# Sharing the odd half-tile of the last product between two batches, and four column groups for a one-column DFT

## The chip, the cores and the metric

One core of one Trainium2 chip. The metric is device time in microseconds (us) of one launch. Eleven executions of the kernel before in one set of rounds lay between 1286.47 and 1290.47 us, 0.3% apart, in another between 1286.91 and 1292.74, 0.5%. All runs quoted here were graded fast. In profile lines PE is the matmul engine (PEld its weight loads), DVE is VectorE, ACT is ScalarE, POOL is GpSimd, SP issues DMA transfers; L89 is line 89 of the kernel. The *granted clock* is the share of its full speed at which PE was let run.

## The reference, cut to what matters

```python
X = np.fft.fft(np.fft.fft(x, axis=1), axis=2).real       # x: (8, 3136, 256), float32
h = np.maximum(X @ w_in, 0.0)                             # 256 -> 1024
conv = sum(conv_w[k] * hp[:, k:k + 3136, :] for k in range(3))   # 3 taps along the sequence, hp is h padded
out = (h * (1 / (1 + np.exp(-conv)))) @ w_out             # 1024 -> 256
```

(The convolution is a loop in the original.) The kernel does the sequence DFT with matmuls on folded input and uses the mirror symmetry of the real part: a first product gives h for a position and its mirror image.

Of the kernel before, what the change touches and what calls it, by code (L numbers as in the profile page):

```python
# [34 lines left out]
def kernel(  # L35
# [34 lines left out]
    ebp = ctx.enter_context(tc.tile_pool(name="ebp", bufs=5))  # L70
    asp = ctx.enter_context(tc.tile_pool(name="asp", bufs=2))
# [167 lines left out]
    def units(b):  # L239
# [5 lines left out]
        def even(sn, c):  # L245
            n = HO // 2 + 1 - c
            nh = HO // 2
            cols = slice(c, HE, 2)
            mms = [product((slice(0, P), slice(j * n, (j + 1) * n)), w(2 * sn + c), sn, q, cols, q == qs[0], q == qs[1])
                   for j, qs in enumerate(((3, 1), (2, 0))) for q in qs]  # L250

            def copy(p):
                a_[sn, c] = asp.tile([P, HO], F32, name="as", tag="as")
                nc.scalar.copy(out=a_[sn, c][:, 0:n], in_=p[:, 0:n])

            def fin(p):
                a, bb, t = a_[sn, c], p[:, n:2 * n], PQ[b][sn]
                vt(t[:, 2 * c:Q4 + 1:4], a[:, 0:n], bb, op=ALU.add)
                hi = t[:, M - 2 * c:Q4:-4]
                x0, x1 = (bb[:, 0:nh], a[:, 0:nh]) if sn else (a[:, 0:nh], bb[:, 0:nh])  # L260
                vt(hi, x0, x1, op=ALU.subtract)
            return Unit(b, mms, copy, fin)
# [4 lines left out]
        def odd_even(sn):  # L267
# [3 lines left out]
            def copy(p):  # L271
                a_[sn] = asp.tile([P, HO + QO], F32, name="as", tag="ao")
                nc.scalar.copy(out=a_[sn][:, HO:], in_=p[:, 0:QO])

            def fin(p):
                a, e0, e2 = a_[sn], a_[sn][:, HO:], p[:, QO:2 * QO]
                vt(a[:, 0:QO], e0, e2, op=ALU.add)
                x0, x1 = (e2, e0) if sn else (e0, e2)
                vt(a[:, HO - 1:QO - 1:-1], x0, x1, op=ALU.subtract)
# [14 lines left out]
        def feature():  # L294

            mms = []
            for j, qs in enumerate(((3, 1), (2, 0))):
                for q in qs:
                    for c in range(2):
                        n = HO // 2 + 1 - c  # L300
                        mms.append(product(
                            (slice(32 * c, 32 * c + 1), slice(j * n, (j + 1) * n)),
                            lambda k, q, c=c: ea[b][0:k, c, q:q + 1], 0, q, slice(c, HE, 2), q == qs[0], q == qs[1]))

            def copy(p):
                a_["e"] = asp.tile([P, HO + QO], F32, name="as", tag="ao"), asp.tile([P, HO], F32, name="as", tag="as")
                for c in range(2):
                    n = 2 * (HO // 2 + 1 - c)
                    nc.scalar.copy(out=a_["e"][c][0:1, 0:n], in_=p[32 * c:32 * c + 1, 0:n])
# [22 lines left out]
    def spread(b):  # L332

        for c, ch in enumerate(chunks):
            eb[b, c] = ebp.tile([P, HN], F32, name="eb", tag="eb")[:, 0:ch.k1 - ch.k0]
            nc.sync.dma_start(out=eb[b, c], in_=ed[b:b + 1, ch.k0:ch.k1].to_broadcast([P, ch.k1 - ch.k0]))

# [4 lines left out]
    class Chunk:  # L342
        def __init__(self, c):
            c0 = CUTS[c]
            c1 = CUTS[c + 1] if c + 1 < len(CUTS) else NK
            self.k0, self.k1 = max(c0 - 1, 0), min(c1 + 1, NK)
            n = self.k1 - self.k0
            f0 = 1 if c0 == 0 else 0
            self.front = slice(f0, f0 + n)
            b0, b1 = (1 if c0 == 0 else 0), (n - 1 if c1 == NK else n)  # L350
            self.cols = slice(b0, b1)
            self.back = slice(f0 + n, f0 + n + b1 - b0)
            self.zeros = c0 == 0
            self.w = self.back.stop + (1 if c0 == 0 else 0)
            if c1 == NK:
                runs = [(0, c0, S - 2 * c0 + 1)]
            else:
                runs = [(0, c0, c1 - c0), (f0 + n, S - c1 + 1, c1 - max(c0, 1))]
            self.tiles = [(g + i, r + i, min(P, l - i)) for g, r, l in runs for i in range(0, l, P)]

    chunks = [Chunk(c) for c in range(len(CUTS))]
    HW = max(c.w for c in chunks)
    HN = max(c.k1 - c.k0 for c in chunks)

# [110 lines left out]
    def copies(s):  # L475
# [4 lines left out]
        for i, cols in enumerate((slice(0, n), ch.cols)):  # L480
            act(nb[s][:, i, cols], p[:, cols], AF.Copy, scale=-1.0 if i else 1.0)  # L481

    def combine(s):
# [7 lines left out]
        for i, (to, cols) in enumerate(((h[:, ch.front], slice(0, n)), (h[:, ch.back][:, ::-1], ch.cols))):  # L491
# [13 lines left out]

    def sigmoid(s):

        n = gs[s].shape[1]
        for c in (slice(n // 2, n), slice(0, n // 2)):
            act(gs[s][:, c], gs[s][:, c], AF.Sigmoid)  # L510

    def gate(s):

        g, h = gs[s], hs.pop(s)
        n = g.shape[1]
        m = n // 2
        gt(g[:, m:n], g[:, m:n], h[:, m + 1:n + 1], op=ALU.mult)  # L517
        vt(g[:, 0:m], g[:, 0:m], h[:, 1:m + 1], op=ALU.mult)  # L518

    def mm2(s):  # L520
        b, c, f = s
        tiles = chunks[c].tiles
        for i, (o, r, m) in enumerate(tiles):
            if f == 0 and i % 2 == 0:
                po[b, c, i // 2] = pso.tile([P, 2, D], F32, name="po", tag="po")
            pt = po[b, c, i // 2]
            mm(pt[0:m, i % 2, :], gs[s][:, o:o + m], wout[:, f, :],
               f == 0 and i % 2 == 0, f == NF - 1)
            if f == NF - 1 and (i % 2 or i == len(tiles) - 1):
                del po[b, c, i // 2]  # L530
                osb = osp.tile([P, 2, D], F32, name="os", tag="os")
                for j in range(i - i % 2, i + 1):
                    _, r, m = tiles[j]
                    nc.scalar.copy(out=osb[0:m, j % 2], in_=pt[0:m, j % 2])  # L534
                    nc.sync.dma_start(out=rows[b * S + r:b * S + r + m, :], in_=osb[0:m, j % 2])
# [10 lines left out]
    for i, u in enumerate(us):  # L546
# [5 lines left out]
        if i == 4:  # L552
            spread(0)
# [18 lines left out]
    for b in range(1, B):  # L572
# [22 lines left out]
        at(cs[-1] - 2, "load", lambda b=b: spread(b))  # L595
# [100 lines left out]
```

## The kernel before: what the change and the argument touch

The kernel is a software pipeline of 256 *steps* (8 batches x 4 chunks of the sequence x 8 groups of 128 hidden features). In each cycle a step's first product runs on PE, the next ones have their taps and gates, and the last product (`po`) of the step three behind runs on PE. The DFT of the next batch is cut in units that are slipped in between.

```python
for t in range(n + LAG):                      # cut: guards
    sigmoid(steps[t - 2])                     # ScalarE, two halves
    products(steps[t + 1]); copies(steps[t + 1])
    run("act")                                # a DFT unit's copies out of PSUM (ScalarE)
    combine(steps[t])                         # VectorE: h of a position and of its mirror
    run("load")                               # loads of x
    run("dve")                                # a DFT unit's sums, the row transfer, POOL's row work
    ...
    other_taps(steps[t - 1])                  # VectorE
    gate(steps[t - 2])                        # h * sigmoid: one half on POOL, one on VectorE
    mm2(steps[t - LAG])                       # PE: the last product
    run("pe")                                 # a DFT unit's matmuls
```

A batch's last product has 3136 rows. The kernel before cuts them into 25 tiles: 23 of 128 rows, one of 127 and one of 65. (With the cut of the chunks moved by a column, as in the change, they are 24 of 128 and one of 64.) Feature D/2 of the DFT is one column that fits in no other unit; its sums are done on POOL in one partition ("row work"):

```python
def feature():                                # one column of weights, two column groups of PE
    for j, qs in enumerate(((3, 1), (2, 0))):
        for q in qs:
            for c in range(2):                # cut: the operands
                mms.append(product((slice(32 * c, 32 * c + 1), slice(j * n, (j + 1) * n)), ...))
    def copy(p):                              # ScalarE, two copies
        for c in range(2):
            nc.scalar.copy(out=a_["e"][c][0:1, 0:n], in_=p[32 * c:32 * c + 1, 0:n])
    def fin(p):                               # POOL, 1 partition
        for c in range(2):
            gt(t[:, 2 * c:Q4 + 1:4], a, bb, op=ALU.add)
            gt(t[:, M - 2 * c:Q4:-4], a[:, 0:nh], bb[:, 0:nh], op=ALU.subtract)
        nc.gpsimd.tensor_scalar(out=t[:, 3:NK:4], in0=t[:, 3:NK:4], scalar1=-1.0, ...)
        nc.sync.dma_start(out=ed[b:b + 1, :], in_=t)
def row():                                    # a 6 KB transfer that POOL's sums are added beside
    nc.sync.dma_start(out=er[b], in_=PQ[b][1][P - 1:P, :])
```

Note the order: row work is issued in `run("dve")`, ahead of `gate` in the same cycle. All of the row work and half of the gate are on POOL, which takes them in this order: in batch 4 the row work from 777.22 us on, the gate at 783.02.

## Time and profile before

| | before |
|---|---|
| time | 1289.94 us, median of 3 |
| span of the profiled execution | 1288.0 us |
| start-up until the first step | 81.4 us |
| batches 1 to 6, from the start of one to the start of the next | 146 to 152 us |

The prediction shows the busy lines and the stretches that it uses. In lists of waits the columns are total idle time, number of times and the longest. This is the list of what PE waited for in the kernel before; the columns are total idle time, number of times and the longest:

```profile
PE po L89 <- DVE g L518: 13.7, 27, 1.6
PE po L89 <- POOL g L517: 12.7, 10, 2.1
```

PE waits nearly as long for POOL's half of the gate, in only ten places, as for VectorE's half in twenty-seven. In seven of the ten (11.4 us) POOL's row work stands in front of the gate; the other three, 0.4 us each, come a step later.

### The profile page before, as it was taken

To read this page: it belongs to the slowest core of one execution; us is meant where nothing else is said; L and a number is where in the kernel's file an instruction comes from. 1 tells how busy PE (TensorE), PEld (TensorE's weight loads), DVE (VectorE), ACT (ScalarE), POOL (GpSimd) and SP (SyncE) were. 2 spreads that over 40 slices of the span, in tenths; PEclk is the share of its full clock that TensorE was granted. 3 is DMA by queue.
4 is the path that set the end of the run, shared out by engine and by line. 5 is a ranking of instruction groups with operands and counts; after the bars stand their busy time and mean duration, and the time that the engine had idled before them with its cause. 6 is when DMAs were issued, how large, how long until landed. Compare 5 with 4: busy or idle time off the path is not lost.

```text
span 1288.0 us, 15443 instructions
## 1 busy us (share of the span) xinstructions
PE 1198.0 (93%) x4914; PEld 898.6 (70%) x4914; DVE 1153.2 (90%) x1664; ACT 880.2 (68%) x1814; POOL 404.1 (31%) x507
## 2 busy tenths in 40 slices
PE   0758999999999999999999999999999999999998
PEld 0535677777677766777677776777677777777776
DVE  6869998998989988898899988998999878898996
ACT  0216766777668766777667776777767777777885
POOL 2414524241523334232513225141322213222222
PEclk9868999999999999999999999999999999999999
DMA  7701202020211102020202103020010001100101
GB/s 226 191 26 39 88 26 87 13 78 25 88 38 44 55 30 76 25 78 25 72 29 63 40 25 100 26 77 5 22 50 26 27 25 44 32 6 22 33 26 44
DMA packets 46842, 66.04 MB, mean 51 GB/s; under 512 B 5600, under 2 KB 35196, under 8 KB 46504
## 3 DMA queue, kind: packets, MB, share of 16 engines
q1 hardware_dynamic: 41012, 49.80, 12.5%
q0 software_dynamic: 5120, 12.85, 3.4%
q10 hardware_dynamic: 628, 2.40, 0.6%
q8 instruction: 38, 0.62, 0.2%
q14 instruction: 44, 0.36, 0.1%
HBM read 39.24 MB, written 25.74 MB: 50 GB/s over the span
## 4 chain that ended last, share of the span: by engine, by line
PE 69%; DVE 17%; issue 4%; ACT 4%; DMA 3%; POOL 2%; DVEq 0%; SPq 0%; ACTq 0%; POOLq 0%
PE po L89 43%; PE pb L89 10%; PE pa L89 9%; PE pd L89 7%; DVE g L504 4%; DVE h L492 2%; DVE g L518 2%; ACT nb L481 2%; DMA dm<-dft_dim_dram 1%; POOL er L319 1%; DVE w L174 1%; DVE xh L147 1%; DVE w L175 1%; DVE xh L158 1%; ACT g L510 1%
## 5 line engine op out<-in xcount | busy, mean ns | idle before, releaser
L89 PE MATMUL po<-wout,g 128*128 128x256 f32 (+2 forms) x3200 | 740.1, 381 | 26.6 <-DVE g L518 13.7
L89 PEld LDWEIGHTS po<-wout,g 128*128 128x128 f32 (+2 forms) x3200 | 597.3, 188 | 190.4 <-DVE g L518 43.4
L504 DVE SCALAR_TENSOR_TENSOR g<-h,cw,g 128x770 f32<-128x770 f32 (+2 forms) x512 | 556.9, 1088 | 11.0 <-ACT g L498 1.5
L517 POOL TENSOR_TENSOR g<-g,h 128x385 f32<-128x385 f32 (+1 forms) x256 | 239.5, 937 | 755.2 <-ACT g L510 571.7
L510 ACT ACTIVATE g<-g 128x385 f32<-128x385 f32 (+3 forms) x512 | 244.1, 527 | 187.6 <-DVE g L504 187.3
L481 ACT ACTIVATE nb<-pb 128x386 f32<-128x386 f32 (+4 forms) x512 | 225.5, 494 | 121.8 <-PE pb L89 120.9
L492 DVE CUSTOM_DVE_ANT_0 h<-pa,nb 128x386 f32<-128x386 f32 (+4 forms) x512 | 265.2, 560 | 15.8 <-PE pa L89 10.0
L498 ACT ACTIVATE g<-h,cw 128x770 f32<-128x770 f32 (+2 forms) x256 | 243.7, 952 | 0.0
L89 PE MATMUL pa<-pt,G 128*128 128x386 f32 (+2 forms) x512 | 213.7, 498 | 9.0 <-ACT pa L466 9.0
L89 PE MATMUL pb<-qt,G 127*128 127x386 f32 (+2 forms) x512 | 215.1, 501 | 4.7 <-ACT nb L481 4.7
L518 DVE TENSOR_TENSOR g<-g,h 128x385 f32<-128x385 f32 (+2 forms) x256 | 155.2, 606 | 5.3 <-ACT g L510 5.3
L466 ACT ACTIVATE pa<-eb,ge 128x386 f32<-128x386 f32 (+2 forms) x256 | 153.9, 601 | 8.2 <-DMA eb<-ed 8.0
L89 PEld LDWEIGHTS pa<-pt,G 128*128 128x128 f32 x512 | 97.4, 191 | 83.3 <-issue 19.8
L89 PE MATMUL pd<-tab,w 99*128 99x196 f32 (+2 forms) x448 | 118.6, 374 | 0.0
L89 PEld LDWEIGHTS pb<-qt,G 127*128 127x128 f32 x512 | 94.0, 191 | 32.0 <-ACT nb L481 7.9
L122 POOL DMA_INDIRECT xh<-in_x_dram,idx x64 | 88.0, 1374 | 16.4 <-issue 13.7
L89 PEld LDWEIGHTS pd<-tab,w 99*128 99x128 f32 (+1 forms) x448 | 83.2, 190 | 13.5
L534 ACT COPY os<-po 128x256 f32<-128x256 f32 (+2 forms) x200 | 60.1, 393 | 16.4 <-DMA out_dram<-os 8.6
L89 PE MATMUL po<-win,dm 128*128 128x512 f32 x8 | 6.5, 994 | 39.2 <-DMA dm<-dft_dim_dram 39.2
L147 DVE TENSOR_TENSOR xh<-xh 98x1020 f32<-98x1020 f32 (+1 forms) x32 | 43.0, 1353 | 0.0
L158 DVE TENSOR_TENSOR xh<-xh 98x1024 f32<-98x1024 f32 (+1 forms) x32 | 41.2, 1294 | 0.1
L89 PEld LDWEIGHTS po<-win,dm 128*128 128x128 f32 x8 | 2.5, 330 | 42.3 <-issue 41.3
(84 smaller groups left out, 373.0 us busy)
## 6 DMA issues: line engine op xcount, KB each, us to landing
out_dram<-os SPq DMA_DIRECT2D x184, 128.0 KB
xh<-in_x_dram SPq DMA_DIRECT2D x16, 784.0 KB
eb<-ed SPq DMA_DIRECT2D x16, 193.0 KB
tab<-dft_seq_dram SPq DMA_DIRECT2D x4, 601.8 KB
raw<-in_moe_w_in_dram ACTq DMA_DIRECT2D x2, 1024.0 KB
raw<-in_moe_w_out_dram SPq DMA_DIRECT2D x1, 2048.0 KB
eb<-ed SPq DMA_DIRECT2D x8, 209.0 KB
eb<-ed SPq DMA_DIRECT2D x8, 192.5 KB
```

Of the source, the lines that this page charges most:

```text
L89: nc.tensor.matmul(o, l, r, start=start, stop=stop, skip_group_check=True)
L122: nc.gpsimd.indirect_dma_start(out=xh[b, h][0:NP, 4 + m].rearrange("p q d -> p (q d)"), out_offset=None, in_=bass.AP(tensor=x.tensor, offs ...
L147: vt(a[:, :, :, 1:D], a[:, :, :, 1:D], r[:, :, :, D - 1:0:-1], op=ALU.add)
L466: act(pa[s][:, 0:n], eb[b, c], AF.Copy, scale=ge[:, f:f + 1])
L481: act(nb[s][:, i, cols], p[:, cols], AF.Copy, scale=-1.0 if i else 1.0)
L492: nc.vector._custom_dve(TENSOR_ADD_SAT, out=to, in0=a[:, cols], in1=c[:, i, cols], s0=BIG, s1=0.0)
L498: act(gs[s], hs[s][:, 0:n], AF.Copy, scale=cw[:, 0, s[2]:s[2] + 1])
L504: stt(out=g, in0=h[:, k:k + n], scalar=cw[:, k, f:f + 1], in1=g, op0=ALU.mult, op1=ALU.add)
L510: act(gs[s][:, c], gs[s][:, c], AF.Sigmoid)
L517: gt(g[:, m:n], g[:, m:n], h[:, m + 1:n + 1], op=ALU.mult)
L518: vt(g[:, 0:m], g[:, 0:m], h[:, 1:m + 1], op=ALU.mult)
L534: nc.scalar.copy(out=osb[0:m, j % 2], in_=pt[0:m, j % 2])
```

## The change

Its intent: the 64 left-over rows of two batches share one tile (49 tiles for two batches, not 50), gathered by VectorE in a small `left` tile; and the eight one-column matmuls of feature D/2 (sixteen instructions in the trace, which is what is counted below) go to four column groups of PE in place of two. The cut of the chunks moves by a column, and the small tiles of the DFT become equal, to make room.

```diff
-            for j, qs in enumerate(((3, 1), (2, 0))):
-                for q in qs:
+            for i in range(2):
+                for j, qs in enumerate(((3, 1), (2, 0))):
                     for c in range(2):
                         n = HO // 2 + 1 - c
-                        mms.append(product((slice(32 * c, 32 * c + 1), slice(j * n, (j + 1) * n)), ...))
+                        o = 32 * (2 * j + c)
+                        mms.append(product((slice(o, o + 1), slice(0, n)), ...))
@@ copy: four copies of half the length in place of two @@
@@ gate @@
+        if r.start < r.stop:
+            vt(left[:, f, b % 2 * LEFT:(b % 2 + 1) * LEFT], g[:, r], h[:, r], op=ALU.mult)
@@ mm2 @@
+        if ch.last and b % 2:
+            tiles.append((left[:, f], [(i * LEFT, b - 1 + i, ch.rest[1], LEFT) for i in range(2)]))
@@ and for each stored tile @@
+                    for p0, b_, r, m in tiles[j][1]:
+                        nc.sync.dma_start(out=rows[b_ * S + r:b_ * S + r + m, :], in_=osb[p0:p0 + m, j % 2])
```

More of the change, by code (lines that the diff above doesn't have):

```diff
@@ L69 @@
     erp = ctx.enter_context(tc.tile_pool(name="erp", bufs=1))
-    ebp = ctx.enter_context(tc.tile_pool(name="ebp", bufs=5))
-    asp = ctx.enter_context(tc.tile_pool(name="asp", bufs=2))
+    ebp = ctx.enter_context(tc.tile_pool(name="ebp", bufs=4))
+    asp = ctx.enter_context(tc.tile_pool(name="asp", bufs=4))
     pqp = ctx.enter_context(tc.tile_pool(name="pqp", bufs=2))
@@ L252, in copy @@
             def copy(p):
-                a_[sn, c] = asp.tile([P, HO], F32, name="as", tag="as")
+                a_[sn, c] = asp.tile([P, HO + 2], F32, name="as", tag="as")
                 nc.scalar.copy(out=a_[sn, c][:, 0:n], in_=p[:, 0:n])
@@ L271, in copy @@
             def copy(p):
-                a_[sn] = asp.tile([P, HO + QO], F32, name="as", tag="ao")
-                nc.scalar.copy(out=a_[sn][:, HO:], in_=p[:, 0:QO])
+                a_[sn], a_["e0"] = [asp.tile([P, HO + 2], F32, name="as", tag="as") for _ in range(2)]
+                nc.scalar.copy(out=a_["e0"][:, 0:QO], in_=p[:, 0:QO])
             def fin(p):
-                a, e0, e2 = a_[sn], a_[sn][:, HO:], p[:, QO:2 * QO]
+                a, e0, e2 = a_[sn], a_["e0"][:, 0:QO], p[:, QO:2 * QO]
                 vt(a[:, 0:QO], e0, e2, op=ALU.add)
@@ L296, in feature @@
             mms = []
-            for j, qs in enumerate(((3, 1), (2, 0))):
-                for q in qs:
+            for i in range(2):
+                for j, qs in enumerate(((3, 1), (2, 0))):
                     for c in range(2):
                         n = HO // 2 + 1 - c
-                        mms.append(product(
-                            (slice(32 * c, 32 * c + 1), slice(j * n, (j + 1) * n)),
-                            lambda k, q, c=c: ea[b][0:k, c, q:q + 1], 0, q, slice(c, HE, 2), q == qs[0], q == qs[1]))
+                        o = 32 * (2 * j + c)
+                        mms.append(product((slice(o, o + 1), slice(0, n)),
+                                           lambda k, q, c=c: ea[b][0:k, c, q:q + 1], 0, qs[i],
+                                           slice(c, HE, 2), i == 0, i == 1))
             def copy(p):
-                a_["e"] = asp.tile([P, HO + QO], F32, name="as", tag="ao"), asp.tile([P, HO], F32, name="as", tag="as")
-                for c in range(2):
-                    n = 2 * (HO // 2 + 1 - c)
-                    nc.scalar.copy(out=a_["e"][c][0:1, 0:n], in_=p[32 * c:32 * c + 1, 0:n])
+                a_["e"] = [asp.tile([P, HO + 2], F32, name="as", tag="as") for _ in range(2)]
+                for j in range(2):
+                    for c in range(2):
+                        n = HO // 2 + 1 - c
+                        o = 32 * (2 * j + c)
+                        nc.scalar.copy(out=a_["e"][c][0:1, j * n:(j + 1) * n], in_=p[o:o + 1, 0:n])
             def fin(p):
@@ L330, in units, with spread @@
         return begin, [odd_even(1), odd(1), even(1, 0), even(1, 1), feature(), odd_even(0), odd(0), even(0, 0), even(0, 1)], row
-    def spread(b):
-        for c, ch in enumerate(chunks):
+    def spread(b, cs):
+        for c in cs:
+            ch = chunks[c]
             eb[b, c] = ebp.tile([P, HN], F32, name="eb", tag="eb")[:, 0:ch.k1 - ch.k0]
@@ L344, in __init__ @@
             c0 = CUTS[c]
-            c1 = CUTS[c + 1] if c + 1 < len(CUTS) else NK
-            self.k0, self.k1 = max(c0 - 1, 0), min(c1 + 1, NK)
+            self.last = c + 1 == len(CUTS)
+            c1 = NK - 1 if self.last else CUTS[c + 1]
+            self.k0, self.k1 = max(c0 - 1, 0), min(c1 + 2, NK)
             n = self.k1 - self.k0
-            f0 = 1 if c0 == 0 else 0
-            self.front = slice(f0, f0 + n)
-            b0, b1 = (1 if c0 == 0 else 0), (n - 1 if c1 == NK else n)
-            self.cols = slice(b0, b1)
-            self.back = slice(f0 + n, f0 + n + b1 - b0)
-            self.zeros = c0 == 0
-            self.w = self.back.stop + (1 if c0 == 0 else 0)
-            if c1 == NK:
-                runs = [(0, c0, S - 2 * c0 + 1)]
-            else:
-                runs = [(0, c0, c1 - c0), (f0 + n, S - c1 + 1, c1 - max(c0, 1))]
-            self.tiles = [(g + i, r + i, min(P, l - i)) for g, r, l in runs for i in range(0, l, P)]
+            self.zeros = c0 == 0
+            f0 = 1 if self.zeros else 0
+            nf = c1 + 1 - self.k0
+            b0, b1 = max(c0, 1) - self.k0, n - 1 if self.last else n
+            self.fcols, self.cols = slice(0, nf), slice(b0, b1)
+            self.front = slice(f0, f0 + nf)
+            self.back = slice(f0 + nf, f0 + nf + b1 - b0)
+            self.w = self.back.stop + f0
+            if self.last:
+                runs = [(0, c0, S - 2 * c0)]
+            else:
+                runs = [(0, c0, c1 - c0), (f0 + nf, S - c1, c1 - c0)]
+            self.tiles = [(g + i, r + i, P) for g, r, l in runs for i in range(0, l - LEFT, P)]
+            self.rest = (runs[0][2] - LEFT, runs[0][1] + runs[0][2] - LEFT)
+    LEFT = P // 2
+    assert B % 2 == 0 and all(c % P == 0 for c in CUTS) and (S - 2 * CUTS[-1]) % P == LEFT
     chunks = [Chunk(c) for c in range(len(CUTS))]
@@ L363 @@
     HN = max(c.k1 - c.k0 for c in chunks)
+    left = const.tile([P, NF, P], F32, name="left")
     def narrow(dst, raw, ng):
@@ L479, in copies @@
         nb[s] = nbp.tile([P, 2, HN], F32, name="nb", tag="nb")
-        for i, cols in enumerate((slice(0, n), ch.cols)):
+        for i, cols in enumerate((ch.fcols, ch.cols)):
             act(nb[s][:, i, cols], p[:, cols], AF.Copy, scale=-1.0 if i else 1.0)
@@ L490, in combine @@
             nc.gpsimd.memset(h[:, 0:ch.w:ch.w - 1], 0.0)
-        for i, (to, cols) in enumerate(((h[:, ch.front], slice(0, n)), (h[:, ch.back][:, ::-1], ch.cols))):
+        for i, (to, cols) in enumerate(((h[:, ch.front], ch.fcols), (h[:, ch.back][:, ::-1], ch.cols))):
             nc.vector._custom_dve(TENSOR_ADD_SAT, out=to, in0=a[:, cols], in1=c[:, i, cols],
@@ L504, in other_taps, with shares @@
             stt(out=g, in0=h[:, k:k + n], scalar=cw[:, k, f:f + 1], in1=g, op0=ALU.mult, op1=ALU.add)
+    def shares(s):
+        ch = chunks[s[1]]
+        w = ch.w - 2
+        n = ch.rest[0] if ch.last else w
+        return slice(0, n // 2), slice(n // 2, n), slice(n, w)
     def sigmoid(s):
-        n = gs[s].shape[1]
-        for c in (slice(n // 2, n), slice(0, n // 2)):
+        v, p, r = shares(s)
+        for c in (slice(p.start, r.stop), v):
             act(gs[s][:, c], gs[s][:, c], AF.Sigmoid)
     def gate(s):
-        g, h = gs[s], hs.pop(s)
-        n = g.shape[1]
-        m = n // 2
-        gt(g[:, m:n], g[:, m:n], h[:, m + 1:n + 1], op=ALU.mult)
-        vt(g[:, 0:m], g[:, 0:m], h[:, 1:m + 1], op=ALU.mult)
+        b, c, f = s
+        g, h = gs[s], hs.pop(s)[:, 1:]
+        v, p, r = shares(s)
+        gt(g[:, p], g[:, p], h[:, p], op=ALU.mult)
+        vt(g[:, v], g[:, v], h[:, v], op=ALU.mult)
+        if r.start < r.stop:
+            vt(left[:, f, b % 2 * LEFT:(b % 2 + 1) * LEFT], g[:, r], h[:, r], op=ALU.mult)
     def mm2(s):
         b, c, f = s
-        tiles = chunks[c].tiles
-        for i, (o, r, m) in enumerate(tiles):
+        ch = chunks[c]
+        tiles = [(gs[s][:, o:o + m], [(0, b, r, m)]) for o, r, m in ch.tiles]
+        if ch.last and b % 2:
+            tiles.append((left[:, f], [(i * LEFT, b - 1 + i, ch.rest[1], LEFT) for i in range(2)]))
+        for i, (w, to) in enumerate(tiles):
             if f == 0 and i % 2 == 0:
@@ L526, in mm2 @@
             pt = po[b, c, i // 2]
-            mm(pt[0:m, i % 2, :], gs[s][:, o:o + m], wout[:, f, :],
-               f == 0 and i % 2 == 0, f == NF - 1)
+            mm(pt[:, i % 2, :], w, wout[:, f, :], f == 0 and i % 2 == 0, f == NF - 1)
             if f == NF - 1 and (i % 2 or i == len(tiles) - 1):
@@ L532, in mm2 @@
                 for j in range(i - i % 2, i + 1):
-                    _, r, m = tiles[j]
-                    nc.scalar.copy(out=osb[0:m, j % 2], in_=pt[0:m, j % 2])
-                    nc.sync.dma_start(out=rows[b * S + r:b * S + r + m, :], in_=osb[0:m, j % 2])
+                    nc.scalar.copy(out=osb[:, j % 2], in_=pt[:, j % 2])
+                    for p0, b_, r, m in tiles[j][1]:
+                        nc.sync.dma_start(out=rows[b_ * S + r:b_ * S + r + m, :], in_=osb[p0:p0 + m, j % 2])
         gs.pop(s)
@@ L552 @@
         if i == 4:
-            spread(0)
+            spread(0, range(len(chunks)))
         for g in late_w[i::len(us)]:
@@ L594 @@
             at(cs[i + 1], "dve", u.fin)
-        at(cs[-1] - 2, "load", lambda b=b: spread(b))
+        at(cs[-1] - 2, "load", lambda b=b: spread(b, range(len(chunks) - 1)))
+        at(per * b + 1, "load", lambda b=b: spread(b, [len(chunks) - 1]))
     LAG = 3
```

## The prediction

> **What bounds the kernel now.** I read the page first (busy shares, 40 slices), then PE and VectorE in order of time, then the waits of VectorE, then one list of my own: the distance between the starts of consecutive first-product matmuls (one step of the pipeline each, 256 steps, 32 a batch).
>
> ```profile
> PE 1198.0 (93%) x4914; PEld 898.6 (70%) x4914; DVE 1153.2 (90%) x1664; ACT 880.2 (68%) x1814; POOL 404.1 (31%) x507
> ...
> PE   0758999999999999999999999999999999999998
> ...
> DVE  6869998998989988898899988998999878898996
> ```
>
> After two slices of start-up (weights, tables, the DFT of batch 0, to about 81 us) PE is nearly full, but VectorE is close behind. So PE work removed counts only where VectorE has room.
>
> PE's price list is start to start, because the rows overlap:
>
> ```profile
> 1138.47 3.18 PE L89 MATMUL po<-wout,g 128*128 128x256 f32 x14
> 1141.49 0.81 PE L89 MATMUL pb<-qt,G 127*128 127x385 f32 x2
> ...
> 1243.50 2.75 PE L89 MATMUL po<-wout,g 128*128 128x256 f32 x12
> 1246.08 0.87 PE L89 MATMUL pb<-qt,G 127*128 127x418 f32 x2
> ```
>
> Seven tiles hold PE for 1141.49 - 1138.47 = 3.02 us, six for 2.58: a tile of the last product (two instructions) costs 0.432 us, whether its weights have 128 or 65 columns. A last-chunk step is therefore 3.02 + 4 x 0.35 = 4.43 us, other steps 3.89.
>
> VectorE in the last chunk of batch 4:
>
> ```profile
> 834.81 0.52 DVE L258 TENSOR_TENSOR pt<-as,pd 128x196 f32<-128x196 f32 x1 [0.58 <-ACT as L254]
> ...
> 842.52 0.59 DVE L518 TENSOR_TENSOR g<-g,h 128x416 f32<-128x416 f32 x1
> 843.03 1.09 DVE L492 CUSTOM_DVE_ANT_0 h<-pa,nb 128x418 f32<-128x418 f32 x2
> 843.17 3.29 PE L89 MATMUL po<-wout,g 128*128 128x256 f32 x14 [0.20 <-DVE g L518]
> 844.03 2.23 DVE L504 SCALAR_TENSOR_TENSOR g<-h,cw,g 128x833 f32<-128x833 f32 x2
> 846.17 0.59 DVE L518 TENSOR_TENSOR g<-g,h 128x416 f32<-128x416 f32 x1
> ...
> 870.75 0.36 DVE L277 TENSOR_TENSOR as<-as,pd 128x196 f32<-128x196 f32 x1 [1.23 <-ACT as L273]
> ```
>
> VectorE waits at 834.2 for a DFT unit's copy and not again until 869.5: 35 us without a gap. Inside, PE at 843.17 starts the instant VectorE's gate is done. So VectorE sets the pace here and PE has only a little slack; VectorE itself has 1.2 us over PE at the end of the stretch. Batches 2 and 4 look alike. In batch 0 VectorE has no gap from 230.8 to 291.4. Batch 6 is different: no folds are left, VectorE's cycle from 1134.58 to 1138.22 is 3.64 us, below PE.
>
> [...]
> - [...] a 256-column row reads 379 ns and recurs every 216, so I used starts.
> - [...] the 16 D/2 instructions of batch 0 start in pairs 2 to 7 ns apart, pair after pair every 0.173 us. Four groups are shown by no run here.
> - [...] For the 416-wide gate [...] 843.03 - 842.52 = 510 ns. [...]
> - [...] the pair of taps takes 2.23 us alone and 2.84 beside a POOL gate at 856.10. VectorE's pace is thus a little elastic.
>
> **The change part by part.**
>
> (a) *Tiles.* 25 tiles x 8 features x 8 batches = 1600 matmuls become 1568: 32 x 0.432 = 13.8 us less PE work, all of it in the last chunk of batches 0, 2, 4, 6 (3.46 us each). Odd batches keep seven tiles. What arrives at the end:
> - Batch 6: PE's step becomes 3.99, then 3.89; VectorE's 3.64 becomes 3.74 (see b). PE still leads: about 3.3.
> - Batches 2 and 4: the step before the VectorE stretch gains 0.43. Inside, I moved each PE start by 0.43 a step against each gate's end plus (b): PE runs into the gate at each second or third step, and at 865.5 it is 0.5 us early. About 0.5 each, 1.0 in all, where PE alone would give 6.9.
> - Batch 0: 0.43 before its stretch, then VectorE-bound with 0.6 to 0.8 added: -0.2.
> Sum 4.1.
>
> (b) *The left-over multiply.* 64 new VectorE operations of 128x64: [...] the 416-wide gate shrinks to 384, -33 ns. Net +0.1 us in each last-chunk step of every batch, 6 us of VectorE work. Batches 0, 2, 4, 6 are counted in (a). In odd ones PE has 4.43 us steps, but batches 1, 3 and 5 stall on VectorE there (0.5 to 1.0 us at single steps), and those stalls grow by two or three steps' worth: -0.8. Batch 7 hides it.
>
> (c) *Output buffers.* Seven tiles need four output tiles of three buffers:
>
> ```profile
> ACT os L534 <- DMA out_dram<-os: 2.8, 1, 2.8
> PEld pb L89 <- ACT nb L481: 1.6, 1, 1.6
> PE pb L89 <- ACT nb L481: 1.2, 1, 1.2
> ```
>
> That is 1157 to 1165 us, the end of batch 6: ScalarE waits 2.8 us for an output DMA to land, and the step on PE loses 1.40. Six tiles need three buffers: +1.3. In the other batches this wait is 0.9 us and hidden.
>
> (d) *Feature D/2.* Eight matmuls of one column. Now they alternate between two groups[...]; in one step (batch 1's DFT) they take eight rounds of 0.173 us, split as 2, 3, 3 over three steps (later batches) 2 + 4 + 4. With four groups: 2 + 2 + 2, or four rounds. Saving 4 x 0.175 = 0.7 us a batch, 4.9 over the seven in the loop; batch 0's is in the start-up, where VectorE sets the end, worth nothing. But what follows it is a chain to POOL:
>
> ```profile
> 772.42 0.72 SPq L328 DMA_DIRECT2D er<-qt  x1
> 776.51 0.96 ACT L309 COPY as<-pd 1x394 f32<-1x394 f32 x2
> 777.22 1.00 POOL L317 TENSOR_TENSOR er<-as 1x197 f32<-1x197 f32 x1 [6.42 <-DMA er<-qt]
> 780.49 2.64 POOL L319 TENSOR_SCALAR er<-er 1x392 f32<-1x392 f32 x1
> 783.02 0.85 POOL L517 TENSOR_TENSOR g<-g,h 128x385 f32<-128x385 f32 x1
> ```
>
> POOL's gate stands behind 5.7 us of row work, and PE stalls some 2.3 us on that gate. The row work starts by the later of ScalarE's copies and the row DMA. Where the DMA is last (here), an earlier PE only waits longer. I give 0.6 to batch 1's unit, 0.3 to the next, 0.2 to each of three, 0.5 and 0.7 to the last two: +2.7. ScalarE has four copies of half the length in place of two; its first POOL-ready pair is the third copy, worth 0.2 us, in these allowances.
>
> (e) *Wider chunks.* 385 and 386 columns become 386 and 387: four instructions x 0.83 ns x 192 steps = -0.6; counted -0.5.
>
> (f) *Pools.* One spread buffer less, the last chunk's row loaded seven steps later; its reader is some twenty steps, 80 us, away. Nothing. The four equal small buffers are each two units from reuse. Nothing.
>
> Sum: 4.1 - 0.8 + 1.3 + 2.7 - 0.5 = 6.8 us. From the median of 1289.9 that is 1283; as VectorE's elasticity under POOL may give a microsecond more, I predict 1282.
>
> **The rivals.**
> 1. *PE alone counts.* 13.8 + 4.9 + 1.3 - 0.6 = 19.4 us, 1270.5. For it: PE 93% busy, most of the last chain. Against it: VectorE's gapless stretches just where three of four tile savings fall.
> 2. *VectorE becomes the bound.* The 6 us of new VectorE work all land and only batch 6 gains: 1288 or above. For it: VectorE 90% busy, and 99% from 1200 to 1250 us. Against it: the latter is mostly lengthening by POOL while PE keeps its 3.89.
> 3. *Four groups don't overlap.* Then (d) is 0 or the added copies cost 0.1 to 0.3 us a batch: 1285 to 1287. Against it: pairs do overlap now. Or the POOL chain is fully led by PE and the whole 4.9 arrives: 1280.
>
> **Range and chances.** My sum lies a third of the way from rival 2 to rival 1; small shifts of stalls across eight batches may add up to 3 us either way. 1274 to 1288 should hold it eight times in ten. 2% is 25.8 us, beyond even rival 1: faster 0.02. Slower by 2% would need a new wait in nearly each step, which the unchanged order of the side work does not suggest: 0.02. Within: 0.96.
>
> **What would show it.** Last-chunk steps of batch 6 at 3.9 to 4.0 us and no output-buffer wait at its end (a, c). In batches 2 and 4 more PE idle put down to the VectorE gate than before, 1 to 2 us each, and a stretch shorter by under 1 us (a). The 128x64 multiply at 0.13 us start to start (b). D/2 instructions starting four within some 10 ns, six in 0.35 us in place of 0.70 (d), with PE's stall on POOL's gate longer by 0.2 to 0.5 us in the middle batches. I would be wrong if batches 2 and 4 shrink by 3 us each, if the span of VectorE's busy time does not grow by some 5 us, or if the start-up moves by over a microsecond.

Start to start (medians from 110 us on) the multiply takes 0.135 us in the kernel after, the 416-wide gate 0.502 in the kernel before and the 384-wide one 0.469 in both: net 0.10 us a step; VectorE's cycle in batch 6 is 3.71 us after (1135.28 to 1138.99), where 3.74 was forecast. The 0.83 ns a column of (e) compares with 327 and 353 ns between the matmuls of 386 and of 418 columns before, 0.81 a column.

## The result, and the profile after

1285.12 us (median of 4, 1283.83 to 1286.31) against 1290.42 us (4 runs): ratio 0.9957, 95% interval 0.994 to 0.9975, that is 5.5 us faster. (Ratios are the mean time of one kernel's fast runs over that of the other's in the same rounds, so not quite the ratio of the medians.) Predicted were 1282 and "within 2%", and the range 1274 to 1288 holds it. So the total was right; the parts were not all.

From the page after, busy times, then the slices of PE:

```profile
PE 1182.6 (92%) x4850; PEld 891.0 (70%) x4850; DVE 1153.8 (90%) x1728; ACT 880.9 (69%) x1826; POOL 396.1 (31%) x507
...
PE   0758999999999999999899999999999999999998
```

PE has 64 matmuls and 15.4 us less to do, but the span is 5.9 us shorter. One slice near the middle now reads 8. PE's waits after:

```profile
PE po L89 <- DVE g L537: 19.7, 37, 1.6
PE po L89 <- POOL g L536: 15.5, 9, 2.7
```

Both have grown: +6.0 us for VectorE's gate, +2.8 for POOL's. My list of step durations (distance between the starts of first products, as in the prediction) gives the difference per batch, after minus before; the column "tile part" is the first experiment below against the same trace.

| stretch, us | after - before | tile part - before |
|---|---|---|
| batch 0 without its first chunk | -1.33 | -1.36 |
| batch 1 | -0.56 | -0.19 |
| batch 2 | +0.53 | -0.49 |
| batch 3 | -0.17 | -0.21 |
| batch 4 | -0.50 | -0.50 |
| batch 5 | +1.42 | -0.03 |
| batches 6 and 7 | -4.82 | -4.67 |
| last PE instruction to the end | +1.41 | +1.27 |

(I leave out start-up and the first eight steps, 1.9 us shorter: start-up varied from 79.0 to 82.7 us between runs of kernels that are alike there.) The last-chunk steps of batch 6 run over into batch 7 by the pipeline's lag, so I take the two together. The same lag puts part of the gain of batches 2 and 4 into the rows of batches 3 and 5. Counted from the first last-chunk step of a batch to the ninth step of the next, the tile part is 1.4, 0.6, 0.6 and 4.7 us shorter in batches 0, 2, 4 and 6 (1.35 us of the 4.7 are an output-buffer wait, see below), and batches 1, 3 and 5 change by -0.04, -0.01 and +0.20 us.

Feature D/2, batch 4. Before is in the prediction, to which two lines are to be added, the D/2 matmuls and the PE wait at the end of that chain (2.04 us, where the prediction says some 2.3):

```profile
774.01 0.85 PE L89 MATMUL pd<-tab,ea 98*1 98x196 f32 x6
...
783.93 1.56 PE L89 MATMUL po<-wout,g 128*128 128x256 f32 x6 [2.04 <-POOL g L517]
```

The same chain after (start, duration, in brackets the idle time before and what ended it):

```profile
768.93 0.73 SPq L331 DMA_DIRECT2D er<-qt  x1
...
770.19 0.52 PE L89 MATMUL pd<-tab,ea 98*1 98x196 f32 x6
...
772.36 1.29 ACT L312 COPY as<-pd 1x197 f32<-1x197 f32 x4
...
773.87 0.86 POOL L320 TENSOR_TENSOR er<-as 1x197 f32<-1x197 f32 x1 [6.55 <-DMA er<-qt]
...
777.01 2.63 POOL L322 TENSOR_SCALAR er<-er 1x392 f32<-1x392 f32 x1
779.53 0.86 POOL L536 TENSOR_TENSOR g<-g,h 128x385 f32<-128x385 f32 x1
...
780.45 1.56 PE L89 MATMUL po<-wout,g 128*128 128x256 f32 x6 [2.71 <-POOL g L536]
```

Two readings. The six D/2 instructions take 0.52 us in place of 0.85, so PE gained what was predicted. But POOL starts when the row transfer has landed, 4.94 us after its issue (before: 777.22 - 772.42 = 4.80), not when PE is done; the PE stall grows from 2.04 to 2.71 us, by just the two savings of 0.33 us that this batch has. The gain is given back in full, two steps later.

In batches 2 and 5 more than that is given back. The windows around the stall of batch 2 (columns: stretch, length, busy times; then the granted PE clock, DMA share, GB/s):

```profile
472.00:482.00 10.00, 7.63 (x35) 5.28 (x34) 8.82 (x12) 7.87 (x18) 6.33 (x6) 1.00 0.22 77
482.00:486.40 4.40, 4.08 (x11) 3.15 (x12) 4.07 (x5) 2.09 (x6) 3.87 (x4) 0.61 0.57 179
```

After the stall the granted clock is 0.61 over 4.4 us. In the records it is halved from 482.68 us on for 3.41 us: 256-column matmuls recur every 0.427 us, not every 0.216. The same happens at 929.83 us in batch 5; each costs 1.6 to 1.7 us. The kernel before has no such place after 110 us in its profile. The clock keeps to a grid: in both profiles each stretch of one granted clock from 45 us on, but for the last, is a whole number of 3.413 us long (halved ones 3.41 to 23.89 us, the longest of all 1177.6 = 345 x 3.413), and the two here begin 447.15 us apart, 131 x 3.413.

How much idle time it takes can be read from the 14 traces. Cut each into windows of 3.413 us, on the grid on which its halved stretches begin, and add up the time in each window in which no matmul record runs (from 105 us on, without the last 12 us). All nine windows with 1.99 us or more were followed by half the clock, so was one with 1.89, and no other, of up to 1.95, was. In the changed kernel the stalls of batches 2 and 5 lie whole in one window (2.68 and 1.99 us); the longer one of batch 4 lies across two, with at most 1.90 us in one. So in these traces the halved clock goes with the idle time within one window, not with the length of the stall, and where a stall falls on the grid is chance. The kernel before's idlest window had 1.65 us, but two other kernels with two column groups, below, met such windows. The mean clock of the timed runs says that the changed kernel meets more of them: 0.983 to 0.984 in its four, 0.984 to 0.988 (mean 0.987) in the 33 of the kernel before beside the experiments. One halved stretch takes 0.0013.

### The profile page after: what moved, and what is told of

It reads as the page before. It is cut to its first block, busy times and chain, and to the rows that moved or that the text cites. A ratio compares the mean times of both kernels' runs of the same rounds, so it can differ in the third digit from the quotient of the medians.

```text
span 1282.1 us, 15552 instructions
## 1 busy us (share of the span) xinstructions
PE 1182.6 (92%) x4850; PEld 891.0 (70%) x4850; DVE 1153.8 (90%) x1728; ACT 880.9 (69%) x1826; POOL 396.1 (31%) x507
## 4 chain that ended last, share of the span: by engine, by line
PE 63%; DVE 21%; issue 7%; ACT 5%; POOL 2%; DMA 2%; DVEq 0%; SPq 0%; POOLq 0%; ACTq 0%
PE po L89 38%; PE pb L89 10%; PE pa L89 8%; PE pd L89 6%; DVE g L516 6%; DVE h L504 3%; DVE g L537 3%; ACT nb L493 2%; DVE xh L147 1%; ACT g L529 1%; POOL er L322 1%; DVE w L174 1%; DVE xh L163 1%; DVE xh L158 1%; DVE w L175 1%
## 5 line engine op out<-in xcount | busy, mean ns | idle before, releaser
L89 PE MATMUL po<-wout,g 128*128 128x256 f32 x3072 | 715.6, 382 | 35.2 <-DVE g L537 19.7
L89 PEld LDWEIGHTS po<-wout,g 128*128 128x128 f32 x3072 | 579.6, 190 | 195.6 <-DVE g L537 55.9
L516 DVE SCALAR_TENSOR_TENSOR g<-h,cw,g 128x770 f32<-128x770 f32 (+1 forms) x512 | 554.1, 1082 | 10.6 <-ACT g L510 1.5
L529 ACT ACTIVATE g<-g 128x385 f32<-128x385 f32 (+2 forms) x512 | 244.2, 527 | 197.5 <-DVE g L516 197.1
L493 ACT ACTIVATE nb<-pb 128x386 f32<-128x386 f32 (+3 forms) x512 | 225.8, 494 | 109.8 <-PE pb L89 108.5
L504 DVE CUSTOM_DVE_ANT_0 h<-pa,nb 128x386 f32<-128x386 f32 (+3 forms) x512 | 265.0, 559 | 14.0 <-PE pa L89 9.0
L510 ACT ACTIVATE g<-h,cw 128x770 f32<-128x770 f32 (+1 forms) x256 | 243.5, 951 | 0.2 <-DVE h L504 0.2
L89 PE MATMUL pa<-pt,G 128*128 128x387 f32 (+2 forms) x512 | 214.1, 499 | 7.2 <-ACT pa L478 7.2
L89 PE MATMUL pb<-qt,G 127*128 127x387 f32 (+2 forms) x512 | 217.1, 505 | 3.6 <-ACT nb L493 3.6
L478 ACT ACTIVATE pa<-eb,ge 128x387 f32<-128x387 f32 (+2 forms) x256 | 154.1, 602 | 7.6 <-DMA eb<-ed 7.4
```

What stands on the lines that cost most here:

```text
L89: nc.tensor.matmul(o, l, r, start=start, stop=stop, skip_group_check=True)
L478: act(pa[s][:, 0:n], eb[b, c], AF.Copy, scale=ge[:, f:f + 1])
L493: act(nb[s][:, i, cols], p[:, cols], AF.Copy, scale=-1.0 if i else 1.0)
L504: nc.vector._custom_dve(TENSOR_ADD_SAT, out=to, in0=a[:, cols], in1=c[:, i, cols], s0=BIG, s1=0.0)
L510: act(gs[s], hs[s][:, 0:n], AF.Copy, scale=cw[:, 0, s[2]:s[2] + 1])
L516: stt(out=g, in0=h[:, k:k + n], scalar=cw[:, k, f:f + 1], in1=g, op0=ALU.mult, op1=ALU.add)
```

## The experiments

Two theories at the outset. *Theory:* the tiles bring what was predicted, and the feature's gain is swallowed since PE waits for POOL's gate behind row work that starts by something other than PE. *Rival:* VectorE sets the pace in most of the batch (PE's wait for its gate grew most), and the added multiply and ScalarE's copies take the gain.

### The tile part alone

The changed kernel with the feature as before:

```diff
-                        o = 32 * (2 * j + c)
-                        mms.append(product((slice(o, o + 1), slice(0, n)), ...))
+                        mms.append(product((slice(32 * c, 32 * c + 1), slice(j * n, (j + 1) * n)), ...))
@@ and two copies of 2 n columns in place of four of n @@
```

> The changed kernel with the D/2 feature back in two column groups and two copies (tiles, left-over multiply and pools stay changed). Theory now, from the two traces: the D/2 part gave back all its 0.67 us a batch in PE's wait for POOL and lost some 2 us more, so the tiles alone are as fast as the whole change or faster: 1283 to 1284 us, ratio to before 0.994 to 0.995. Rival, the prediction's sum: D/2 saves 2.7 us, so the tiles alone stand at 1286 to 1288.

1283.3 us (1282.01 to 1284.63), ratio 0.9961 (0.9948 to 0.9974): 5.0 us. This is all of the change's gain within the intervals. The table above shows where: 3.3 us at the end of batch 6 (seven steps of 0.43 and one of 0.25; the row has 1.35 more of the output-buffer wait), 1.4 in batch 0, 0.5 in batches 2 and 4 each. This run also has the new chunk cut, buffers and later load; no run takes these apart from the shared tile.

### The feature part alone

```diff
@@ kernel before @@
-                        mms.append(product((slice(32 * c, 32 * c + 1), slice(j * n, (j + 1) * n)), ...))
+                        o = 32 * (2 * j + c)
+                        mms.append(product((slice(o, o + 1), slice(0, n)), ...))
@@ and four copies of n columns @@
```

> The kernel before with the D/2 feature in four column groups and four copies alone. Theory now: PE's 0.67 us a batch is eaten by a longer wait for POOL: ratio 1.000 to 1.002, the D/2 steps 0.33 us shorter twice a batch and the PE stall on POOL's gate longer by 0.3 to 0.7 us a batch[...]. Rival, the prediction: -2.7 us (0.998). Rival, PE alone: -4.9 us (0.996).

1286.63 us, ratio 0.9991 (0.9977 to 1.0004): between nothing and 3 us, which does not exclude the prediction's 2.7. By the step list its batches are 0.1 us shorter together (without the output-buffer wait), with one halved clock in batch 2, after a stall of 2.72 us; the stalls of 2.70 and 2.71 us in batches 3 and 4 had none (see the grid above). The four groups do overlap. My list of the starts of the six instructions, in ns from the first:

```
before, batch 4:   0   6  173  179  347  520
after,  batch 4:   0   7   13  173  182  187
```

All sixteen of batch 0 take 0.88 us in place of 1.57. So the first half of rival 3 of the prediction is out, and yet little or nothing arrives.

### The copies alone

```diff
-                    n = 2 * (HO // 2 + 1 - c)
-                    nc.scalar.copy(out=a_["e"][c][0:1, 0:n], in_=p[32 * c:32 * c + 1, 0:n])
+                    for j in range(2): nc.scalar.copy(... columns j * n to (j + 1) * n ...)
```

> The kernel before with its two D/2 groups, but each of ScalarE's two copies split in two, so four copies as in the change. If the third copy delays POOL's row work, POOL starts 0.5 us later in the batches where ScalarE releases it, and the time grows by 1 to 3 us (1.001 to 1.002). If the copies cost nothing: 1.000.

1286.92 us, ratio 0.9987 (0.9974 to 1.0001): no cost in the total. In its trace single steps moved both ways by 0.4 to 0.9 us and the clock halved once (342.8 us). The expected delay is there all the same: in batches 5 and 6 POOL's row work starts 3.52 us after the D/2 matmuls, before 3.04, so four copies cost it 0.48 us. What hides it is that in batches 2 to 5 the row work is shorter, 4.9 us where it took 5.4 to 5.9: the second subtraction takes 0.6 us in place of 1.3 to 1.4. So here the length of POOL's operations goes with when they start; what lengthens them was not tested here.

### More output buffers

The kernel before with four output buffers in place of three (and the changed kernel's small tiles for room).

> The kernel before with four output buffers in place of three (room made by the changed kernel's equal small buffers). Theory: ScalarE's 2.8 us wait at the end of batch 6 goes and PE's step there is 1.3 us shorter: 1288.5 to 1289.3 us, ratio 0.999. Rival: the wait is hidden or turns into another, 1.000.

1285.67 us (1284.93 to 1289.62), ratio 0.9977 (0.9964 to 0.999). This does not show that the buffers are worth it. Its profiled execution was the slowest of the five, with two halved clocks after stalls of 2.04 and 2.06 us. ScalarE's waits for a free output buffer: the first line is the feature part alone, the second the kernel before with later row work (an experiment below); both have three buffers and seven tiles as before. The third is the changed kernel.

```profile
ACT os L537 <- DMA out_dram<-os: 6.7, 8, 1.0
```

```profile
ACT os L542 <- DMA out_dram<-os: 8.4, 8, 2.5
```

```profile
ACT os L556 <- DMA out_dram<-os: 3.0, 4, 0.9
```

The single wait of 2.8 us that the prediction took its term (c) from is not there in the first, nor in the trace with the copies alone, but the second has it again (2.5 us). The step that took 5.24 us in the kernel before takes 4.97 there and 3.89 in the other twelve traces. So with three buffers and seven tiles two of four traces have the late transfer, and with six tiles or four buffers none of ten. The small gain of this run may be its removal or the medians of a few runs; I can't tell.

### POOL's row work later

The test of the theory: the row work is cut in three and put behind POOL's gate, over three steps, in the changed kernel, in the kernel before, and in the tile part.

```diff
-            at(cs[i + 1], "dve", u.fin)
+            for j, f in enumerate(u.parts):            # part(0), part(1), last
+                at(cs[i + 1] + j, "late", f)
@@ the loop @@
         if 0 <= t - 2 < n:
             gate(steps[t - 2])
+        run("late")
```

> The changed kernel, with POOL's row work of the D/2 feature (five instructions, some 5.7 us) cut in three parts that are issued over three steps, each behind POOL's gate of its step instead of ahead of it. Theory (the gain of the four column groups is swallowed because PE waits for POOL's gate behind the row work, and the halved clock in batches 2 and 5 follows from that wait): the stall of 1.7 to 2.7 us in each of seven batches goes, so 10 to 17 us faster than the changed kernel, 1268 to 1275, and no stretch with the granted clock halved after such a stall. Rival (VectorE sets the pace around these steps and the wait for POOL only stands where a wait for VectorE would come): no more than 3 us faster, 1282 to 1285.

> The kernel before, with the same later row work on POOL. Theory: the wait for POOL's gate is as costly there (12.7 us of PE idle in its profile), so 8 to 15 us faster than before, 1274 to 1281. It also tells what the whole change is worth once this wait is gone: the theory says more than the 5 us it brings now, 7 to 10 us (4.9 us of PE time in feature D/2 plus the tiles); the rival says 5 us or less.

> The tile part of the change alone (two column groups, two copies), with the same later row work on POOL. Against the run of the whole change with later row work this is the four column groups alone. Theory (their 4.9 us of PE time was only hidden by POOL): 2 to 5 us slower than that run. Rival (the four groups are worth nothing since VectorE has the pace): equal within 1 us.

| later row work in | us | ratio to before | 95% |
|---|---|---|---|
| the changed kernel | 1265.48 | 0.9816 | 0.9804 to 0.9829 |
| the kernel before | 1273.70 | 0.9885 | 0.987 to 0.9899 |
| the tile part | 1268.78 | 0.9842 | 0.9829 to 0.9855 |

The changed kernel gains (0.9957 - 0.9816) x 1289 = 18 us, a little beyond the expectation; the other two came as expected. PE's waits, with later row work:

```profile
PE po L89 <- DVE g L545: 20.1, 37, 1.6
...
PE po L89 <- POOL g L544: 0.7, 3, 0.3
```

The wait for POOL falls from 15.5 to 0.7 us, and there is no halved clock after 110 us and before the end in any of the three (I searched all traces for matmuls that recur at twice their normal distance): 14.8 us plus two times 1.65 make 18.1, which is the measured gain. The wait for VectorE's gate does *not* grow. So the rival falls for these places: no wait for VectorE stood behind the one for POOL. POOL's new order in batch 4:

```profile
759.46 0.86 POOL L544 TENSOR_TENSOR g<-g,h 128x385 f32<-128x385 f32 x1 [3.82 <-issue]
762.30 0.81 POOL L319 TENSOR_TENSOR er<-as 1x197 f32<-1x197 f32 x1 [1.97 <-DMA er<-qt]
...
766.94 0.87 POOL L544 TENSOR_TENSOR g<-g,h 128x385 f32<-128x385 f32 x1
```

The gate comes first, and POOL alone waits for the row transfer.

With the wait gone, the whole change is worth 0.9885 - 0.9816, 8.9 us, where it brought 5.5; the tile part 5.5 us (0.9885 - 0.9842) and the four column groups 3.4 us (0.9842 - 0.9816) of the 4.9 that PE saves. Each of these has some 2.5 us either way by the intervals, so that the columns now bring something is clear, and how much more the whole brings is less so. By my step list the other part of it is lost in batches 2, 3 and 4, where 0.5 to 1.0 us come back some five steps later; in batch 3 the trace has PE waiting there 0.24 us for POOL's gate and 0.39 for VectorE's. How much more a still later third part would bring is open.

### The row transfer earlier

Which event starts POOL's row work in the changed kernel? The 6 KB transfer is issued 0.4 us behind a 784 KB load of x on the same queue. The edit issues it one unit earlier, ahead of that load:

```diff
-            if i == 4:
-                at(cs[i + 1], "dve", row)
             at(cs[i + 1], "dve", u.fin)
+            if i == 3:
+                at(cs[i + 1], "dve", row)
```

> The changed kernel as it is, with the 6 KB row transfer that POOL's row work adds to issued a unit earlier, ahead of the 784 KB load that it is queued behind. Theory (in the middle batches this transfer, not PE, starts POOL's row work, so the four column groups can't make it start earlier): the row work starts some 0.5 to 2 us earlier in batches 2, 3 and 4, 2 to 5 us faster than the changed kernel, 1280 to 1283; batches 0, 5 and 6, where ScalarE's copies come last, unmoved. Rival (ScalarE's four copies are the last everywhere): within 1 us of 1285.

1281.3 us, ratio 0.9944 (0.9928 to 0.996) against 0.9957 for the changed kernel: 1.7 us, under the expected 2 to 5, and the intervals overlap. What starts the row work is read from the trace. Batch 4 in it:

```profile
770.82 0.85 POOL L320 TENSOR_TENSOR er<-as 1x197 f32<-1x197 f32 x1 [6.07 <-ACT as L312]
...
775.42 1.62 POOL L536 TENSOR_TENSOR g<-g,h 128x385 f32<-128x385 f32 x1
```

Now ScalarE's copies release POOL. My list, time from the start of the last D/2 matmuls to the start and to the end of POOL's row work, in us:

| batch | 0 | 1 | 2 | 3 | 4 | 5 | 6 |
|---|---|---|---|---|---|---|---|
| before: start | 3.81 | 4.26 | 3.50 | 3.45 | 3.21 | 3.04 | 3.04 |
| before: end | 9.44 | 8.84 | 9.13 | 9.12 | 9.12 | 8.45 | 7.86 |
| after: start | 3.61 | 4.24 | 3.58 | 4.01 | 3.68 | 3.19 | 3.20 |
| after: end | 9.42 | 8.81 | 9.43 | 9.47 | 9.45 | 7.98 | 7.99 |
| transfer earlier: start | 3.61 | 3.25 | 3.20 | 3.20 | 3.20 | 3.20 | 3.20 |
| transfer earlier: end | 9.43 | 7.95 | 7.95 | 7.94 | 7.91 | 7.97 | 7.99 |

With the transfer out of the way the work starts 3.20 us after the matmuls in five batches out of five from batch 2 on and ends 1.5 us earlier in batches 2 to 4. So there the transfer was last. The semaphores in the traces show its landing: in the changed kernel 4.7 to 5.2 us after its issue in batches 2 to 4 and 1.9 in the others, in this run 1.9 in all. In batches 0, 5 and 6 it is ScalarE, and its four copies (1.29 us, before 0.96 for two) cost 0.48 us, more than the 0.33 by which PE is done sooner in that step: the row work of batches 5 and 6 starts 0.15 us later after the start of the matmuls than before.

Of the 1.5 us, 0.4 to 0.8 are the earlier start; the rest is that two of POOL's five operations are shorter (0.9 and 2.0 us in place of 1.3 and 2.6). And PE gets only half: its stall falls from 2.7 to 1.9 us, as POOL's gate behind the row work now takes 1.62 us, not 0.86. In the changed kernel's trace the 784 KB load is issued 0.4 us ahead of the row transfer in batches 2, 3 and 4 alone (at 470.42, 618.29 and 768.53 us), the three in which the 6 KB take 4.7 to 5.2 us to land; once they are ahead of it they take 1.9. Batch 2 lost its halved clock with its shorter stall, too (2.05 us less in one step); batch 5, whose stall is that of the changed kernel (1.99 us), still has one, begun 1.0 us after the stall. Stalls of 1.0 to 2.0 us remain in each batch, which is why later row work brings more.

### What the left-over multiply costs on VectorE

In the changed kernel, last chunk of batch 4:

```profile
842.75 0.55 DVE L537 TENSOR_TENSOR g<-g,h 128x384 f32<-128x384 f32 x1
843.22 0.22 DVE L539 TENSOR_TENSOR left<-g,h 128x64 f32<-128x64 f32 x1
843.35 1.08 DVE L504 CUSTOM_DVE_ANT_0 h<-pa,nb 128x418 f32<-128x418 f32 x2
```

0.13 us start to start, as predicted, though the record reads 0.22. Three runs ask what arrives: the multiply on POOL (`gt` for `vt`, in the changed kernel), and, with later row work, the multiply issued three times, and not at all.

```diff
-            vt(left[:, f, ...], g[:, r], h[:, r], op=ALU.mult)
+            gt(left[:, f, ...], g[:, r], h[:, r], op=ALU.mult)         # run 1: on POOL
+            for _ in range(3): vt(left[:, f, ...], ...)                # run 2: three times
+                                                                       # run 3: none, left filled with zeros once
```

> The changed kernel with the multiply of the left-over 64 columns on POOL instead of VectorE. Theory of the prediction (VectorE sets the pace in the last chunk of batches 0 to 5 and this multiply costs it 0.13 us in each step there): 48 steps x 0.13 us would be 6 us if all of it were on the path; of the three even batches some 3 us should come, 1281 to 1283. Rival (VectorE's pace is elastic, its taps only run longer or shorter beside POOL): within 1 us of the changed kernel, or slower as POOL's second operation collides with the taps.

> The changed kernel with later row work on POOL, and the multiply of the left-over 64 columns issued three times on VectorE (same result): 0.26 us more VectorE work in each last-chunk step. If VectorE sets the pace there in batches 0, 2 and 4 as the prediction had it, these batches lose most of 8 x 0.26 us each and odd ones 1 to 3 us, together 6 to 12 us over the same kernel with one multiply, 1271 to 1277. Rival (it lies in VectorE's slack): within 1.5 us of 1265.5.

> The same with no left-over multiply at all (a wrong result on purpose: the shared tile is filled with zeros once, so the shared rows of all batches come out wrong). It prices the term directly. If the prediction's 0.1 us a step arrives in batches 0 to 5: 2 to 4 us faster than 1265.5. Rival (VectorE waits for something else in these stretches, or is only lengthened by POOL): within 1 us.

On POOL: 1285.38 us, ratio 0.9977 (0.9962 to 0.9991), no gain. There the multiply takes 1.0 us each, so the time does not separate relief of VectorE from new load on POOL; and its profile has two halved-clock stretches. By the step list the last chunks of batches 0, 2 and 4 are 0.4 to 0.5 us shorter, as without the multiply (next run), and that of batch 3 is 0.8 us longer.

None: 1263.94 us, ratio 0.9807 (0.9791 to 0.9822) against 0.9816, its result wrong as intended. That is 1.2 us of the 64 x 0.13 = 8.3 us taken away, within the interval; the traces say 1.5.

Three times: 1313.46 us, 48 us more, and my expectation of 6 to 12 was far off. The dose was: the three take 851.75 - 850.52 = 1.23 us, 1.10 more than one, not 0.26. Each repeat writes the same columns, and the starts are 0.25 us apart, not 0.13. The larger part is another: in 56 of the 64 steps the third one runs beside POOL's gate multiply. It mostly begins 0.15 us after that one, takes 0.79 us in place of 0.22, and ends 0.08 us after it; in the eight steps without POOL beside it the three take 0.65 us. Of 8 x 1.10 = 8.8 us a batch, 5 to 8 us arrive in batches 0 to 6 and 2.7 in batch 7 (1.7 us in batch 0 are a halved clock). So VectorE has a little slack, not much: 0.13 us a step are mostly absorbed, 1.1 us mostly not.

### A larger share of the gate on POOL

A try to beat the best, with later row work:

```diff
-        return slice(0, n // 2), slice(n // 2, n), slice(n, w)
+        m = n * 7 // 16
+        return slice(0, m), slice(m, n), slice(n, w)
```

> A try for a faster version: later row work, and POOL takes 9/16 of the gate in place of half (48 columns, some 0.05 us, less on VectorE in each step). If VectorE's work is what PE waits for (20 us of PE idle put down to its gate): 2 to 5 us faster than 1265.5. Rival (POOL's longer operation stretches VectorE's taps by as much, or PE then waits for POOL): equal or slower.

1269.4 us, ratio 0.9849 (0.9833 to 0.9866): some 4 us slower. VectorE's taps with half on POOL, then with 9/16 (count, busy us, mean ns):

```profile
L524 DVE SCALAR_TENSOR_TENSOR g<-h,cw,g 128x770 f32<-128x770 f32 x384 | 414.8, 1080 | 7.9 <-ACT g L518 1.1
```

```profile
L524 DVE SCALAR_TENSOR_TENSOR g<-h,cw,g 128x770 f32<-128x770 f32 x384 | 427.7, 1114 | 7.8 <-ACT g L518 1.0
```

The taps are 34 ns longer on the mean with the longer POOL operation beside them, two a step, which is more than the 59 ns that the smaller VectorE gate saves (590 to 531 ns); and PE waits 2.2 us for POOL again. So the rival held.

## Why the prediction was right or wrong

The total was right: 1285.1 for 1282, predicted saving 6.8 us, measured 5.5. It was right partly by luck, because misses cancel: 3.5 to 5 us of the sum did not come ((d) 2.2, going by the 0.5 it adds to the tiles, the end 1.3, and (c) 0 to 1.3, by the execution), and 2 to 3 us came that were not in it (batch 0: 1.4 shorter, not 0.2 longer; odd batches: 0.15 longer together, not 0.8).

- **(a) tiles.** Batch 6, 3.3 us: right. Batches 2 and 4, 0.5 to 0.6 each: right, and so is its reason; PE idle at VectorE's gate rose by 6 us, 1.9, 2.2 and 2.1 of them at the last chunks of batches 0, 2 and 4, and in batches 2 and 4 five shortened steps alternate with three lengthened ones. Batch 0: predicted 0.2 slower, measured 1.4 faster; "VectorE-bound" there was too strict; that its operations shrank as well (next point) may be why. PE alone (rival 1) is refuted, VectorE as the only bound (rival 2) too.
- **(b) the multiply.** Its price, 0.13 us, and the net 0.1 were sized right, or nearly, for one operation; its arrival was not. Predicted was 0.8 us of loss in odd batches, on stalls of 0.5 to 1.0 us in three of them; the tile part shows 0.15 us of loss, and batch 5 hardly had such a stall (0.15 us in all). The test "VectorE's busy time grows by some 5 us" failed: 1153.2 to 1153.8. By kind, the mean time times the count gives taps 2.8 us and gates 3.7 us less, and some 5 us of the multiply's 14.0 recorded us lie under the next record. So the term was oversized; that the other VectorE operations were held constant is the likely reason.
- **(c) output buffers, 1.3 us: right for that execution, oversized as a mean.** It was read from one wait in one execution. With three buffers and seven tiles the step is as short in two traces of four, and lost 1.35 and 1.08 us in the others.
- **The end: missed.** The last tile is now a shared one, stored by two transfers. From the start of the last PE instruction to the end of the span it takes 5.50 to 6.08 us in all nine traces with shared tiles, 4.29 to 4.41 in the five without: over a microsecond lost, which the prediction's "batch 7 hides it" passed over. Of the 1.41 us, 1.2 lie between the end of ScalarE's last copy and the end of the last store's issue (0.59 before, 1.82 after, with two issues there in place of one). That the second transfer is the cause is argued from this, not tested.
- **(d) feature D/2.** PE's 0.33 us twice a batch: right. "+2.7 arrives": wrong, by the step that gave an allowance to each batch. Alone it brought 1.2 us (-0.5 to 3), on top of the tiles 0.5, which is within the noise of none. Where the row transfer is last, nothing arrives in the stall (allowed: 0.2 a batch); where ScalarE is, the four copies, put at 0.2 us, cost 0.48; and the longer stalls make a halved clock more likely, which came in two batches, 3.3 us in the profiled execution, and which no rival had. The prediction had the mechanism in its hands ("an earlier PE only waits longer") and still credited a gain.
- **(e), (f).** -0.5 and 0: nothing in the runs speaks against them, nor tests them.

What would have been the larger prize was in the profile before: 12.7 us of wait for a gate that stood behind work with no hurry. Moved, it brings 14.8 us to the kernel before and, with the change, 1265.5 us: 1.8% below the kernel before.

## What to carry to other kernels

Ask of each stall which event releases it before you shorten something upstream: a saving ahead of a wait that a transfer or a third engine ends is paid back at that wait. Where an engine takes work in the order of issue, as POOL did here (the gate at 783.02 us behind the row work in the kernel before, at 759.46 ahead of it in the changed kernel with later row work), put work without a deadline behind the operation that the busiest engine waits for; here that was worth three times the change itself. Don't make a full term of a sum from one odd wait in one execution: look whether other executions have it.
